# Weight pieces of a recurrent attention kernel loaded in rows of 1536 and 1280 bytes instead of 3072 and 3840

## The chip, the cores and the metric

The kernel runs on one core of a Trainium2 chip. The metric is the device time of one execution in microseconds (us); before the change it is 1880.98 us, the median of three runs. Differences below about 0.5% are not told apart from no change.

## What is computed

Two branches over 2048 tokens of width 640 are mixed by a gate. Branch A is attention with 32 heads of 192, run over 64 segments of 32 tokens; the first 8 rows of each segment's output are the memory rows of the next, so the segments form a chain. Branch B is a gated feed-forward layer.

```python
for s in range(n_seg):                                  # 64 segments, one after the other
    xs = x[:, s * seg_len:(s + 1) * seg_len, :].copy()
    h = jnp.concatenate([mem, xs], axis=1)              # 8 memory rows and 32 tokens
    q = jnp.einsum('btd,dhe->bhte', h, Wq)
    k = jnp.einsum('btd,dhe->bhte', h, Wk)
    v = jnp.einsum('btd,dhe->bhte', h, Wv)
    scores = jnp.einsum('bhqe,bhke->bhqk', q, k) * scale
    scores = jnp.where(mask[None, None], scores, -1000000000.0)
    p = _softmax(scores, axis=-1)
    o = jnp.einsum('bhqk,bhke->bhqe', p, v)
    o = jnp.einsum('bhte,hed->btd', o, Wo)
    mem = o[:, :M, :].copy()
    outs.append(o[:, M:, :])
...
return g * a + (1 - g) * b        # b = (gelu(x @ w_gate) * (x @ w_up)) @ w_down
```

## The kernel before

**Stages.** The feed-forward branch comes first (about 165 us), with its result stored in a scratch tensor. After a short stage for the left rows of the first groups the 64 segments follow, from about 180 us on, 26.4 us each on average. Everything is written as one list of operations in program order; a small scheduler (`_Sched`) splits it into one stream for each engine and puts semaphore waits where regions overlap. Each engine runs its stream in order, and so does SP, which issues nearly all DMAs.

**A segment.** The 32 heads are treated as four octets of 8 heads. For an octet, Q and K and V are products of the segment's 640 rows of h, in five slices of 128 (k = 0 to 4), with a weight piece each (`proj`, L1039 and, where the stationary operand is kept, `_matmul_kept`, L226). Then come the transposes of Q and K, scores, softmax, the transpose of p, p times V (`pv_oct`, L1172 and L1174, in products of 32 columns), and the product with Wo (`wo_split` and `wo_part`, L1201 and L1224). `PROG` interleaves the octets by hand: items `("g", i, k)` are the projections of the seven groups in `GROUPS`. Group 4 holds the Q of the fourth octet, group 5 its K, group 6 its V, and `("wo", 3, ...)` its Wo. Even segments take the octets in the order 0, 1, 2, 3, odd segments in the order 3, 2, 1, 0. Other products that fill PE (left rows, L882; left products of Wo) are interleaved too.

**Weight pieces.** A piece of Wq, Wk or Wv is one slice k of one octet: 128 partitions with a contiguous row of 1536 bf16 numbers, 3072 bytes. A piece of Wo is one head pair: 128 partitions with 3 times 640 numbers, which lie together in memory, 3840 bytes. Not all pieces fit: 17 slots are shared by a piece of octet 0 and one of octet 3 (14 of the 15 slices of Q, K and V, `NSQ = 14`, and three pairs of Wo, `NSW = 3`). As soon as the first octet of a segment has used a shared slot, the piece of its other octet is loaded there (`swap_loads`, which calls `load_piece`, L597), to be used by the fourth octet of the same segment. So each segment but the first loads 1 + 4 K pieces, 4 Q pieces, 5 V pieces and 3 Wo pieces, in the order K, Q (4), K (4), V (5), Wo (3): 14 x 393,216 + 3 x 491,520 bytes = 6.98 MB. The load of a slot waits for the PE that used it last, and PE waits for its landing. `load_piece` also makes the first loads of all resident pieces, by `load_residents`; nine pieces used once at the start are loaded to a temporary place by `load_tmp`, at another line.

**SP's stream around them.** In a segment SP issues, in this order: the first piece of K, the Q and K and V pieces as their slots come free, between them the output store of the segment before (L951) and the x load for the next (L704), later the Wo pieces, the load of the next segment's left Q and K (`stg_load`, L932), the loads of branch B's rows (L942, L947), and in most segments a store of left Q and K (L893).

Of the kernel before, what the change touches and what calls it, by code (L numbers as in the profile page):

```python
# [231 lines left out]
def _build(nc, A_x, A_mem0, A_Wq, A_Wk, A_Wv, A_Wo, seg_len, w_gate, w_up, w_down,  # L232
# [34 lines left out]
    S_ = _Sched(nc)  # L267
# [84 lines left out]
    def bview(o, nbytes, plo=0, phi=128):  # L352
        return arena[plo:phi, o // 2:(o + nbytes) // 2]
# [4 lines left out]
    def sreg(o, nbytes, plo=0, phi=128):  # L358
        return Rg("sb", o, o + nbytes, plo, phi)
# [129 lines left out]
    def piece_src(key):  # L489
        if key[0] == 3:  # L490
            return Wo2[:, key[1]]
        m, o_, k = key
        return (Wq2, Wk2, Wv2)[m][:, k, OW * o_:OW * (o_ + 1)]

    def piece_size(key):
        return GO if key[0] == 3 else GQ

    def piece_view(key, o):
        if key[0] == 3:
            return bview(o, GO).rearrange("p (c n) -> p c n", n=Dm)  # L500
        return bview(o, GQ)
# [59 lines left out]
    res_off = {}  # L561
# [8 lines left out]
    r_res = {key: sreg(o, piece_size(key)) for key, o in res_off.items()}  # L570
# [23 lines left out]

    def load_piece(key, name):
        loaded[slot_id[key]] = key
        S_.add("sp", lambda e: e.dma_start(piece_view(key, res_off[key]), piece_src(key)), writes=[r_res[key]],  # L597
               dma_sem="slot%d" % slot_id[key], name="%s %s" % (name, key))

    def piece(seg, key):  # L600
# [9 lines left out]
    def swap_loads(seg, item):  # L610
        if item[0] == "g" and item[1] == 0 and 0 < item[2] < KT - 1:
            later.extend(key for key in done_keys if key[0] == 1)
            done_keys[:] = [key for key in done_keys if key[0] != 1]
        elif later:
            done_keys[:] = sorted(done_keys + later, key=lambda key: key[:1] + key[2:])
            del later[:]
        for key in done_keys:
            other = swap_in.get(key)
            if other is None or (other in partner) == (seg % 2 == 0):
                continue  # L620
            load_piece(other, "swap s%d" % seg)
        del done_keys[:]
# [11 lines left out]
    def load_residents(cls, pick=lambda key: True):  # L634
        for key in first:
            if slot_class[key] == cls and pick(key):
                load_piece(partner[key] if key in tmp_off else key, "res")
# [39 lines left out]
    for h in range(NH):  # L677
        for w_, sb_, rw_, nm in ((w_gate, wg_sb, r_wg, "wg"), (w_up, wu_sb, r_wu, "wu")):
            S_.add("sp", lambda e, h=h, w_=w_, sb_=sb_: e.dma_start(
                sb_[h], w_.rearrange("(p k) f -> p k f", p=128)[:, :, FH * h:FH * (h + 1)]),  # L680
                writes=[rw_[h]], dma_sem="%s%d" % (nm, h))
# [758 lines left out]
```

## Time and profile before

| What | Value | Where from |
|---|---|---|
| Time, three runs | 1888.29, 1880.98, 1879.60 us | the runs |
| Time of the profiled execution | 1876.1 us | its own run |
| Its span | 1874.4 us, granted clock 0.992 | the page's first line, the view of cores |
| Segments, start to start of their piece loads | 26.4 us mean, 23.9 to 29.1 us | issues of L597 in the trace |
| Piece loads by L597 | 335 V, 330 K, 268 Q, 205 Wo: 1138 | the view of line L597 |
| Packets over 2 KB | 263,040 - 116,224 = 146,816 | the page, part 2 |

The span runs from the first to the last instruction; 1.7 us of the execution lie outside it. The packets over 2 KB are the weight pieces, 1147 loads with 128 rows each: the 1138 of L597 and the nine of `load_tmp`. In the pages, PE is the matrix engine, PEld its weight loads, DVE, ACT and POOL the vector, scalar and general engines, and SP the queue that issues DMAs. "issue" as a releaser means that the engine waited for nothing that the profile shows.

### The profile page before, as it was taken

What the parts mean: (1) busy time and instruction counts of PE and PEld (TensorE: products, weight loads), DVE (VectorE), ACT (ScalarE), POOL (GpSimd) and SP (SyncE); (2) the same over time, 40 slices, a digit from 0 to 9 for tenths busy, and PEclk for the clock granted to TensorE, in tenths of its full rate; (3) what the DMA queues carried; (4) which work ended last, traced back from release to release, by engine and by line L of the source; (5) the groups of instructions that cost most, each with busy time, mean ns of one, the idle gap of its engine ahead of it and who ended that gap; (6) DMA issues with size and microseconds to landing.
All of it is one profiled execution on the core that took longest, in us unless ns stands there. A gap on an engine that the chain in (4) does not pass through costs nothing.

```text
span 1874.4 us, 86233 instructions
## 1 busy us (share of the span) xinstructions
PE 1612.4 (86%) x42253; PEld 838.3 (45%) x34573; DVE 958.3 (51%) x2932; ACT 792.3 (42%) x1835; POOL 319.0 (17%) x1099
## 2 busy tenths in 40 slices
PE   9999889888888889888878989888888888888887
PEld 4544444444444444444434444444444444444444
DVE  2223555555555555555555555555555555555554
ACT  2223444434344444434444444444444444444433
POOL 1100111111111112111211112111111111111211
PEclk9999999999999999999999999999999999999999
DMA  9726787868777887868777887878777887878776
GB/s 341 261 56 213 295 319 274 302 247 314 288 256 275 316 314 261 297 259 319 279 252 289 320 301 261 297 276 317 279 255 291 320 303 259 293 279 313 270 268 266
DMA packets 263414, 524.72 MB, mean 280 GB/s; under 512 B 97384, under 2 KB 116224, under 8 KB 263040
## 3 DMA queue, kind: packets, MB, share of 16 engines
q1 hardware_dynamic: 259912, 516.11, 75.9%
q8 instruction: 300, 4.92, 1.0%
q10 hardware_dynamic: 3128, 3.09, 0.5%
q14 instruction: 74, 0.61, 0.1%
HBM read 498.00 MB, written 21.11 MB: 277 GB/s over the span
## 4 chain that ended last, share of the span: by engine, by line
PE 68%; issue 10%; DVE 10%; DMA 6%; ACT 6%; SPq 0%; DVEq 0%; ACTq 0%
PE ps L1039 19%; PE ps L226 14%; PE ps L1201 8%; DMA arena<-in_A_Wk_dram 3%; PE ps L799 3%; PE ps L802 3%; PE ps L1224 3%; PE ps L1172 3%; PE ps L1093 3%; PE ps L882 2%; PE ps L817 2%; DMA arena<-in_A_Wv_dram 2%; PE ps L1088 2%; PE ps L1080 2%; DVE arena L889 1%
## 5 line engine op out<-in xcount | busy, mean ns | idle before, releaser
L1039 PE MATMUL ps<-arena 128*32 128x384 bf16 x9940 | 753.1, 330 | 89.1 <-DVE arena L1344 50.2
L226 PE MATMUL ps<-arena 128*32 128x384 bf16 x7680 | 601.0, 328 | 15.6 <-ACT arena L887 5.8
L1039 PEld LDWEIGHTS ps<-arena 128*32 128x32 bf16 x9940 | 266.0, 97 | 443.8 <-issue 276.9
L1073 DVE STREAM_TRANSPOSE arena<-arena 128x384 bf16<-128x384 bf16 x512 | 278.9, 564 | 270.0 <-ACT arena L1059 269.6
L1201 PE MATMUL ps<-arena 128*32 128x320 bf16 x6144 | 309.0, 301 | 52.6 <-issue 51.3
L1059 ACT ACTIVATE arena<-ps 128x384 bf16<-128x384 f32 x512 | 236.2, 489 | 194.6 <-PE ps L1039 180.8
L1201 PEld LDWEIGHTS ps<-arena 128*32 128x32 bf16 x6144 | 176.6, 97 | 109.0 <-issue 64.8
L1107 DVE TENSOR_REDUCE arena<-ps 104x4 f32<-104x160 f32 x256 | 83.1, 325 | 199.7 <-PE ps L1093 199.1
L1119 ACT ACTIVATE ps<-ps 104x160 f32<-104x160 f32 x256 | 74.1, 289 | 251.6 <-DVE ps L1109 251.6
L1157 ACT ACTIVATE arena<-ps 128x448 bf16<-128x448 f32 x192 | 104.8, 546 | 172.9 <-PE ps L1144 172.9
L1191 POOL COPY arena<-arena 128x96 bf16<-128x96 bf16 x256 | 68.4, 267 | 583.6 <-ACT arena L1183 461.5
L936 POOL COPY arena<-arena 128x96 bf16<-128x96 bf16 x256 | 69.2, 270 | 527.4 <-PE ps L1093 442.7
L1183 ACT ACTIVATE arena<-ps 128x480 bf16<-128x480 f32 (+1 forms) x256 | 137.9, 539 | 40.5 <-PE ps L1174 33.3
L1062 ACT ACTIVATE arena<-ps 128x384 bf16<-128x384 f32 x256 | 124.8, 487 | 54.2 <-PE ps L1039 54.1
L1172 PE MATMUL ps<-arena 128*32 128x160 bf16 x3072 | 122.8, 235 | 18.4 <-issue 12.6
L882 PE MATMUL ps<-arena 128*32 128x384 bf16 x1280 | 119.1, 330 | 13.5 <-issue 13.4
L1174 PE MATMUL ps<-arena 128*32 128x64 bf16 x3072 | 110.4, 193 | 7.9 <-issue 7.7
L1172 PEld LDWEIGHTS ps<-arena 128*32 128x32 bf16 x3072 | 84.1, 96 | 69.7 <-ACT arena L1062 21.7
L1121 DVE TENSOR_REDUCE arena<-ps 104x4 f32<-104x160 f32 x256 | 82.3, 321 | 59.6 <-ACT ps L1119 53.2
L889 DVE STREAM_TRANSPOSE arena<-arena 128x384 bf16<-128x384 bf16 x128 | 73.7, 576 | 52.4 <-ACT arena L887 51.3
L887 ACT ACTIVATE arena<-ps 128x384 bf16<-128x384 f32 x128 | 62.3, 490 | 65.0 <-DVE arena L889 22.7
L1109 DVE TENSOR_TENSOR ps<-ps,arena 104x160 f32<-104x160 f32 x256 | 85.1, 332 | 8.8
(84 smaller groups left out, 1841.2 us busy)
## 6 DMA issues: line engine op xcount, KB each, us to landing
arena<-in_A_Wk_dram SPq DMA_DIRECT2D x335, 384.0 KB, 7.9
arena<-in_A_Wv_dram SPq DMA_DIRECT2D x335, 384.0 KB, 9.3
arena<-in_A_Wq_dram SPq DMA_DIRECT2D x272, 384.0 KB, 5.6
arena<-in_A_Wo_dram SPq DMA_DIRECT2D x205, 480.0 KB, 7.1
left_qk_scratch<-arena SPq DMA_DIRECT2D x64, 192.0 KB, 2.2
arena<-left_qk_scratch SPq DMA_DIRECT2D x63, 192.0 KB, 7.4
ffn_b_scratch<-arena ACTq DMA_DIRECT2D x16, 160.0 KB, 3.8
arena<-ffn_b_scratch SPq DMA_DIRECT2D x64, 40.0 KB
```

Source lines behind the costliest of these rows:

```text
L226: return e.add_instruction(mybir.InstMatmult(name=nm, start_tensor_calc=like["start"], stop_tensor_calc=stop, tile_size=(128, 32), tile_po ...
L882: fns.append(lambda e, outp=outp, rhs=rhs, j=j: e.matmul(outp, lhs, rhs, start=(k == 0), stop=(k == KT - 1), tile_position=(0, 32 * j)))
L889: S_.add("dve", lambda e: e.transpose(out=dst[:, :, m].rearrange("p q c i -> p c q i"), in_=rowl.rearrange("p (c r) -> p c r", r=L)), read ...
L1039: fns.append(lambda e, outp=outp, rhs=rhs, j=j: e.matmul(outp, lhs, rhs, start=(k == 0), stop=(k == KT - 1), tile_position=(0, 32 * j)))
L1059: S_.add("act", lambda e, m=m, bk=bk: e.activation(out=rows_sb[m], in_=ps[:, bk, 0:384], func=ACTF.Copy), reads=[r_ps[bk]], writes=[r_rows ...
L1062: S_.add("act", lambda e, i=i, bk=bk: e.activation(out=v_sb[i % NVB].rearrange("p (c n) -> p c n", c=3), in_=ps[:, bk, 0:384].rearrange("p ...
L1073: S_.add("dve", lambda e: e.transpose(out=dst[:, :, 0:L], in_=rows_sb[m].rearrange("p (c r) -> p c r", r=L)), reads=[r_rows[m]], writes=[r ...
L1157: S_.add("act", lambda e: e.activation(out=PT, in_=ps[:, bank, 0:PTW + 128], func=ACTF.Copy), reads=[r_ps[bank]], writes=[r_PT], name="pT ...
L1172: return [lambda e: e.matmul(full, v[:, e0:e0 + 32], PTm[:, j // 2], start=True, stop=False, tile_position=(0, 32 * j), skip_group_check=T ...
L1174: lambda e: e.matmul(part, vl[:, e0:e0 + 32], PTl[:, j // 2], start=False, stop=True, tile_position=(0, 32 * j), skip_group_check=True)]
L1183: S_.add("act", lambda e: e.activation(out=apx(u[:, 0, 0, :], [[R, na], [3 * R, 4], [1, R]]), in_=ps[:, A, 0:na * W].rearrange("p (c t r) ...
L1201: fns.append(lambda e, i=i, t=t, j=j, gv=gv: e.matmul(ps[32 * j:32 * j + 32, bank, 0:2 * DJ].rearrange("p (h n) -> p h n", h=2), lhs2[i], ...
```

## The change

The DMA in `load_piece` is given a limit on the contiguous part that one descriptor moves, in bytes. A row of 3072 bytes is then moved as two of 1536, and a row of 3840 bytes as three of 1280. Source, destination, order, semaphores and the number of DMAs stay. All 1138 loads of L597 are affected, the nine of `load_tmp` are not, nor any other DMA.

```diff
     def load_piece(key, name):
         loaded[slot_id[key]] = key
-        S_.add("sp", lambda e: e.dma_start(piece_view(key, res_off[key]), piece_src(key)), writes=[r_res[key]],
+        S_.add("sp", lambda e: e.dma_start(piece_view(key, res_off[key]), piece_src(key), max_dma_last_dim=1536), writes=[r_res[key]],
                dma_sem="slot%d" % slot_id[key], name="%s %s" % (name, key))
```

## The prediction, made before the changed kernel was run

> **What bounds the kernel now.** First the page's busy times, slices and DMA queues.
>
> ```profile
> PE 1612.4 (86%) x42253; PEld 838.3 (45%) x34573; DVE 958.3 (51%) x2932; ACT 792.3 (42%) x1835; POOL 319.0 (17%) x1099
> ...
> DMA  9726787868777887868777887878777887878776
> DMA packets 263414, 524.72 MB, mean 280 GB/s; under 512 B 97384, under 2 KB 116224, under 8 KB 263040
> ...
> q1 hardware_dynamic: 259912, 516.11, 75.9%
> q8 instruction: 300, 4.92, 1.0%
> ```
>
> PE is busy 86% and bounds most of the span. The DMA engines come next at 76%: within a segment they run without a pause and then rest. So the question is where a landing comes last. The list of waits tells how much PE stands for weight pieces:
>
> ```profile
> PEld ps L1039 <- issue: 276.9, 931, 2.3
> ...
> PEld ps L1039 <- DMA arena<-in_A_Wk_dram: 13.7, 28, 1.4
> ...
> PEld ps L1039 <- DMA arena<-in_A_Wv_dram: 6.7, 12, 0.9
> ...
> PE ps L1039 <- DMA arena<-in_A_Wk_dram: 5.3, 12, 1.1
> ```
>
> Columns: us in total, times, longest. These waits are small, some 20 to 30 us, but they show that there is no cover: the timeline of PE has K's matmuls of group 5 starting one by one as pieces land.
>
> ```profile
> 881.68 0.35 PE L1039 MATMUL ps<-arena 128*32 128x384 bf16 x4 [0.49 <-DMA arena<-in_A_Wk_dram]
> 882.65 0.35 PE L1039 MATMUL ps<-arena 128*32 128x384 bf16 x4 [0.62 <-DMA arena<-in_A_Wk_dram]
> 883.63 0.35 PE L1039 MATMUL ps<-arena 128*32 128x384 bf16 x4 [0.23 <-DMA arena<-in_A_Wk_dram]
> ```
>
> Starts 0.97 us apart: the pace of the DMA engines for 384 KB (about 404 GB/s). From the landings and first uses in the trace I took the slack of every piece (first use less landing; about 0.04 us when PE is waiting) in 63 segments. In 23 the smallest slack is below 0.06 us, in 18 above 1 us, in 22 between. The tight pieces are K's in group 5 and the third of Wo.
>
> The other idle time of PE is "issue", with stalls up to 2.3 us. The trace has 300 instruction packets of 16 KB, PE has 76,826 instructions, and 300 x 256 = 76,800: of 136 long stalls that end about 1.4 us after such a packet has landed, 124 come at the same remainder of the instruction count by 256. PE waits for its program. The packet starts 1.06 us (median) after PE entered the block before when the DMA engines rest, and 3.4 us when they move over 350 GB/s; 124 of 130 such stalls (138 us in the segments) are then. So under load the program waits some 2.4 us more, behind weight rows.
>
> **The change part by part.** It removes 933 x 128 rows of 3072 bytes and 205 x 128 of 3840, and adds 2 x 128 and 3 x 128 packets for each: packets go from 263,414 to 435,318. DMA instructions, bytes and order stay. SP's issue should cost nothing more: a store of 512 packets issues in 0.37 us, as a piece of 128 does.
>
> ```profile
> 868.62 0.37 SPq L893 DMA_DIRECT2D left_qk_scratch<-arena  x1
> ...
> 895.58 0.35 SPq L597 DMA_DIRECT2D arena<-in_A_Wk_dram  x1
> ```
>
> SP will stand longer at a full queue, since by estimate 100 to 130 packets an engine fill it (the first loads, issued back to back, land up to 13.9 us after issue: 14 pieces of 8 rows and a completion). Behind it are the output store, the x load and the next left Q and K (L951, L704, L932); they run behind the same pieces on the DMA engines anyway, and land a median of 3.4 us (x) and 3.3 us (left Q and K) before POOL uses them, 1.4 us at the least in the segments for the second. That covers the delays below; without that cover the whole delay of up to 1.4 us a segment would show.
>
> *Price of a split row.* By the packet records the commonest durations are 121 ns (3072 bytes), 149 (3840), 65 (1536) and 55 (1280). By these, a row costs 2 x 65 - 121 = 9 ns or 3 x 55 - 149 = 16 ns more. An engine takes 8 rows of a piece: +72 ns for Q, K or V, +128 for Wo. That is the upper end. But durations of small packets overlap: the 1280-byte rows of w_down land at 51.8 ns each (4.97 us for 96 an engine) and the 768-byte rows of w_gate and w_up at 32.6. The line through these two gives 61.4 ns for 1536; the left Q and K, eight 1536-byte rows an engine, land 486 ns (median) after the last Wo piece, 60 ns each. Sixteen at 61.4 and 7 ns for the completion are 989 ns against 975 to 979 between two V or K pieces now: +12. Without any overhead of size it is 0, the lower end for Q, K and V; against the same line for whole rows (119 ns for 3072) it is +30. I take +20, between the two. For Wo, 24 x 51.8 + 7 = 1250 against 1203 (median): +47; the line gives +61, and I take +50. Nothing in these rows makes a split row cheaper; a gain can come only by the program's wait, below.
>
> [...]
>
> *From pace to time.* The pieces of a segment stand in one queue without a pause, so piece n is late by the sum up to it: at +20 and +50, 0.16 us at the eighth (K), 0.43 us at the third of Wo. A segment grows by the largest of (delay less slack); what follows in it depends on K or Wo and goes late with it, and the next segment's loads start from its end. Over the 63 segments this is 5.0 us, in 27 of them; at 0 and +40 it is 0.3, at +30 and +61 7.9, at +72 and +128 26.5.
>
> *The program.* The loaded time of a segment grows by 14 x 0.020 + 3 x 0.050 = 0.43 us, 27 us over 64 segments. The stalls are now 138 us in about 64 x 18.5 = 1184 us of loaded time: 0.117 us for each. So 3.2 us more.
>
> *Start.* First pieces land over 100 us before use, the last of the start 1.3 us or more: nothing, covered by that slack.
>
> Sum: 5.0 + 3.2 = 8.2 us on the profiled execution's 1876.1 us (span 1874.4, 1.7 outside) = 1884.3. That execution lies 4.9 us under the median of the runs shown; on the median it is 1880.98 + 8.2 = **1889 us**, which I forecast. Its own range is 1881 to 1894 (0.3 to 12.5 us more).
>
> **Rivals.**
>
> *Durations count in full.* Each packet costs its record, +72 and +128 ns. Then pieces pace PE in 43 of 63 segments, for 26.5 us, and the loaded time grows by 1.39 us a segment, 89 us, x 0.117 = 10.4. Sum 37: 1918 us. For it: rows of 3072 now come at exactly their record (8 x 121 = 968 of 975). Against: w_down's and w_gate's rows come faster than their records of 55 and 36 ns.
>
> *The program gets through sooner (the other side).* If what stands ahead of the program's packet is a fixed number of rows, about 20 now, half-size rows halve its 2.5 us. Each stall shrinks by up to 1.3 us, in sum 126 us; PE then reaches K before its pieces do, and with +20 and +50 the same sum over segments leaves a gain of 74 us: 1807 us. It decides from a shortening of about 0.1 us a stall (-6 us net, with 13 gained). For it: the wait is there only under load. Against: where small packets stand in the queue (mean 1.9 KB), the wait is 2.6 to 2.9 us over 35 packets, and where large ones stand 2.5 us over 20; bytes (67 KB an engine) are the same and the count is not. [...]
>
> *No effect, or the split undone.* If two adjacent rows are joined again, or 1536 bytes cost nothing more (60 ns a row, as landed), the time is that of before, 1881 us. Packets of the old size in the records would show the first.
>
> **How the numbers follow.** The forecast has 0.52, the full durations 0.20, the sooner program 0.15, no effect 0.13. Within 0.5% (9.4 us) is what a measurement of this kernel can't tell from no change. The forecast's range lies across that border, and its larger part of the unknown is upward: I split it 0.25 within, 0.27 slower. Slower is 0.27 + 0.20 = 0.47; same 0.25 + 0.13 = 0.38; faster 0.15. The range for 8 in 10 goes from 1868 (a small gain at the program's stalls, and runs like those before at 1879.6) to 1920, just past the full durations; most of the sooner program's 0.15 and some above are left out.
>
> **What will show it.** Packets: 435,318, under 2 KB 433,792. Commonest durations of the new packets near 65 and 55 ns; share of q1 between 76% and 80%. Landings of K pieces 0.98 to 1.01 us apart, of Wo 1.25. PE's waits for K, V and Wo pieces grow from some 30 us to some 35 to 40; idle on "issue" grows by 3 us. The instruction packet under load still starts 3.4 us after its block. It is wrong if that start moves by more than 0.2 us either way, if K's landings stand 1.04 us apart or more, or if SP's longer standing makes x or the left Q and K late.

## The result, and the profile after

The changed kernel took 1929.43 us (median of four runs, 1927.2 to 1943.96) against 1880.29 us for the kernel before (four runs): a ratio of 1.0276, interval 1.0223 to 1.0329. It is slower, by 49 us, where the prediction had 1889 us and a range up to 1920. The profiled execution took 1930.92 us, its span is 1929.2 us.

The page of the changed kernel, its parts on busy times, slices, DMA queues and DMA issues (the last: KB of each, and median us from issue to landing):

```profile
span 1929.2 us, 86214 instructions
...
PE 1641.6 (85%) x42234; PEld 849.5 (44%) x34573; DVE 957.5 (50%) x2932; ACT 793.7 (41%) x1835; POOL 320.2 (17%) x1099
...
DMA  9727878868877888878877888868877897878787
...
DMA packets 435318, 524.72 MB, mean 272 GB/s; under 512 B 97384, under 2 KB 433792, under 8 KB 434944
...
q1 hardware_dynamic: 431816, 516.11, 79.1%
q8 instruction: 300, 4.92, 1.0%
...
arena<-in_A_Wo_dram SPq DMA_DIRECT2D x205, 480.0 KB, 7.8
```

The packets are those of the arithmetic, the bytes are the same, and the share of q1 rose from 75.9% of a shorter span to 79.1% of a longer one: 1422.7 us of engine time became 1526.0. A Wo piece lands 7.8 us after its issue; it was 7.1. PE's busy time rose by 29 us although its instructions did not change. The changed kernel's list of waits (total us, times, longest):

```profile
PEld ps L1039 <- issue: 293.4, 962, 2.3
...
PEld ps L1201 <- issue: 78.3, 58, 2.8
...
PEld ps L1039 <- DMA arena<-in_A_Wk_dram: 18.2, 42, 1.5
...
PEld ps L1039 <- DMA arena<-in_A_Wv_dram: 8.2, 17, 1.0
...
PE ps L1039 <- DMA arena<-in_A_Wk_dram: 5.2, 14, 1.1
...
PEld ps L1224 <- DMA arena<-in_A_Wo_dram: 4.1, 5, 2.1
```

The same line of L1201 in the kernel before:

```profile
PEld ps L1201 <- issue: 64.8, 45, 2.5
```

The waits for pieces grew little (K's on PEld 13.7 to 18.2 us). The waits on "issue" grew more (L1039 276.9 to 293.4, L1201 64.8 to 78.3), and these hold the stalls for the program. Lines of PE and PEld overlap, so the next table takes the time in which both stood, from the trace, by what ended it. (Where two waits end together the choice moves a few us between rows.) Its last rows are from the landings and the clock records.

| | Before | After |
|---|---|---|
| PE and PEld both idle, us | 253.2 | 278.9 |
| of it ended by "issue" | 138.9 | 160.3 |
| of it ended by a Wq, Wk, Wv or Wo piece | 9.5 | 15.6 |
| PE or PEld busy, us (half clock included) | 1613.4 | 1642.5 |
| between landings of two V / K / Wo pieces, median ns | 975 / 979 / 1203 | 1036 / 1054 / 1281.5 |
| instruction packet under over 350 GB/s: start after block entry, median us | 3.42 | 3.75 |
| lost to half clock (half the length of the stretches), us | 16.4 in 8 stretches | 50.9 in 25 |

So the DMA engines need 61 to 75 ns more for a piece of Q, K or V and 78 ns more for one of Wo. In the changed kernel's timeline of PE, a tight stretch of group 5 looks like this (start, us, and in brackets the wait before it):

```profile
899.69 0.35 PE L1039 MATMUL ps<-arena 128*32 128x384 bf16 x4 [0.27 <-DMA arena<-in_A_Wk_dram]
900.75 0.35 PE L1039 MATMUL ps<-arena 128*32 128x384 bf16 x4 [0.31 <-DMA arena<-in_A_Wk_dram]
```

The matmuls start 1.06 us apart instead of 0.97. The stalls for the program are seen in the same timeline, and what follows one of them in the view of windows (us, busy time of PE, PEld, DVE, ACT and POOL, granted clock, DMA share, GB/s):

```profile
1040.76 0.33 PE L1201 MATMUL ps<-arena 128*32 128x320 bf16 x1 [2.13 <-issue]
```

```profile
1034.20:1037.50 3.30, 3.27 (x122) 1.74 (x94) 2.45 (x9) 2.27 (x6) 0.86 (x4) 1.00 1.05 375
1037.50:1040.90 3.40, 1.27 (x35) 0.74 (x31) 1.47 (x5) 0.95 (x3) 0.27 (x1) 1.00 1.06 370
1040.90:1044.30 3.40, 3.40 (x60) 2.29 (x56) 0.00 (x0) 0.54 (x1) 0.00 (x0) 0.50 1.08 365
```

One stall of 2.13 us leaves PE busy 1.27 of 3.40 us (37%), and the next 3.40 us are granted a clock of 0.50. (The counts of matmuls in these windows, 122 and 60, are of different mixes; the matmuls of L1201 alone take 474 ns in the median inside the half-clock stretches and 299 outside.) All half-clock stretches but the last are 3.41 us long, or twice that. PE counts as busy in them: busy time inside the stretches rose from 26.5 to 90.5 us between the two profiles, and outside them it fell by 34.8, so the whole 29 us of added busy time lie there.

### The profile page after: what moved, and what is told of

Read it like the earlier page. It is cut to its first block, busy times and chain, and to the rows that moved or that the text cites. A ratio compares the mean times of both kernels' runs of the same rounds, so it can differ in the third digit from the quotient of the medians.

```text
span 1929.2 us, 86214 instructions
## 1 busy us (share of the span) xinstructions
PE 1641.6 (85%) x42234; PEld 849.5 (44%) x34573; DVE 957.5 (50%) x2932; ACT 793.7 (41%) x1835; POOL 320.2 (17%) x1099
## 3 DMA queue, kind: packets, MB, share of 16 engines
q1 hardware_dynamic: 431816, 516.11, 79.1%
## 4 chain that ended last, share of the span: by engine, by line
PE 66%; issue 10%; DVE 9%; DMA 8%; ACT 6%; SPq 0%; DVEq 0%; ACTq 0%
PE ps L1039 19%; PE ps L226 14%; PE ps L1201 8%; DMA arena<-in_A_Wk_dram 4%; PE ps L802 3%; PE ps L799 3%; DMA arena<-in_A_Wv_dram 3%; PE ps L1172 3%; PE ps L1224 2%; PE ps L1093 2%; PE ps L882 2%; PE ps L817 2%; PE ps L1088 2%; PE ps L1080 2%; DVE arena L889 1%
## 5 line engine op out<-in xcount | busy, mean ns | idle before, releaser
L1039 PE MATMUL ps<-arena 128*32 128x384 bf16 x9940 | 763.0, 334 | 92.8 <-DVE arena L1344 47.9
L1039 PEld LDWEIGHTS ps<-arena 128*32 128x32 bf16 x9940 | 267.7, 98 | 462.8 <-issue 293.4
L1201 PE MATMUL ps<-arena 128*32 128x320 bf16 x6144 | 322.2, 310 | 63.3 <-issue 61.4
L1059 ACT ACTIVATE arena<-ps 128x384 bf16<-128x384 f32 x512 | 236.2, 489 | 204.9 <-PE ps L1039 190.7
L1201 PEld LDWEIGHTS ps<-arena 128*32 128x32 bf16 x6144 | 182.1, 100 | 124.4 <-issue 78.3
L1183 ACT ACTIVATE arena<-ps 128x480 bf16<-128x480 f32 (+1 forms) x256 | 137.9, 539 | 44.2 <-PE ps L1174 37.3
L1062 ACT ACTIVATE arena<-ps 128x384 bf16<-128x384 f32 x256 | 124.9, 488 | 56.2 <-PE ps L1039 56.0
L882 PE MATMUL ps<-arena 128*32 128x384 bf16 x1280 | 118.1, 333 | 13.7 <-issue 13.7
L1172 PEld LDWEIGHTS ps<-arena 128*32 128x32 bf16 x3072 | 86.1, 97 | 69.8 <-ACT arena L1062 22.0
L1174 PEld LDWEIGHTS ps<-arena 128*32 128x32 bf16 x3072 | 84.6, 98 | 18.6 <-issue 12.7
L1139 PE MATMUL ps<-arena 104*32 104x80 bf16 x1024 | 64.4, 205 | 29.7 <-issue 13.7
```

What stands on the lines that cost most here:

```text
L882: fns.append(lambda e, outp=outp, rhs=rhs, j=j: e.matmul(outp, lhs, rhs, start=(k == 0), stop=(k == KT - 1), tile_position=(0, 32 * j)))
L1039: fns.append(lambda e, outp=outp, rhs=rhs, j=j: e.matmul(outp, lhs, rhs, start=(k == 0), stop=(k == KT - 1), tile_position=(0, 32 * j)))
L1059: S_.add("act", lambda e, m=m, bk=bk: e.activation(out=rows_sb[m], in_=ps[:, bk, 0:384], func=ACTF.Copy), reads=[r_ps[bk]], writes=[r_rows ...
L1062: S_.add("act", lambda e, i=i, bk=bk: e.activation(out=v_sb[i % NVB].rearrange("p (c n) -> p c n", c=3), in_=ps[:, bk, 0:384].rearrange("p ...
L1172: return [lambda e: e.matmul(full, v[:, e0:e0 + 32], PTm[:, j // 2], start=True, stop=False, tile_position=(0, 32 * j), skip_group_check=T ...
L1174: lambda e: e.matmul(part, vl[:, e0:e0 + 32], PTl[:, j // 2], start=False, stop=True, tile_position=(0, 32 * j), skip_group_check=True)]
```

## The experiments

All change `load_piece` (L597) of the kernel before. "Idle" below is the time in which PE and PEld both stood; unchanged kernels ran beside each group.

**Which pieces.** The split for Q, K and V alone (first added line), then for Wo alone (second; `key[0]` is 3 for Wo).

```diff
-        S_.add("sp", lambda e: e.dma_start(piece_view(key, res_off[key]), piece_src(key)), writes=[r_res[key]],
+        S_.add("sp", lambda e: e.dma_start(piece_view(key, res_off[key]), piece_src(key), max_dma_last_dim=4096 if key[0] == 3 else 1536), writes=[r_res[key]],
...
+        S_.add("sp", lambda e: e.dma_start(piece_view(key, res_off[key]), piece_src(key), max_dma_last_dim=1536 if key[0] == 3 else 4096), writes=[r_res[key]],
```

> Rows of Q, K and V split, rows of Wo whole. Pace theory (a split row takes an engine longer, everything else follows from the longer transfers): the 14 pieces of a segment land 0.065 us later each, 0.91 us of the 1.14 us that the full change adds to a segment's transfers, so about 39 of its 49 us: 1915 to 1924 us, with landings of K pieces 1.05 us apart and of Wo pieces 1.20 as before. If what counts is the packets in the queue (of 435,318 some 80% of the added ones stay), the same; this run only measures the share of Q, K and V.

> Rows of Wo split into three, all others whole. Pace theory: 3 pieces, 0.078 us each, 0.23 us a segment: about +10 us, 1886 to 1894 us, K landings 0.975 us apart as before. Packet-count theory (each added packet costs the same somewhere else than on the engines): 410 of the 1343 added packets in a thousand per... that is 52,480 of 171,904 added packets, 31%, so +15 us.

Measured: 1915.01 us, ratio 1.0190 (1.0151 to 1.0228), and 1898.51 us, ratio 1.0105 (1.0062 to 1.0147), against 1879.11. Alone the parts give 35.9 and 19.4 us, in sum 55 for 49 together: they add up within their intervals. Landings moved only where rows were split (K 1052 ns and Wo 1197 in the first; K 978 and Wo 1274 in the second). Idle on issue was 164.0 and 157.5 us, idle on pieces 13.9 and 3.7. The first came as expected, at the lower edge of its range. The second was 4 us over the top of the pace theory's range and nearer to the packet-count theory's +15 us, so this run alone does not decide between the two. Wo's split adds 3 x 71 ns = 0.21 us a segment, 14 us in all, and costs 19. PE did not stand longer for pieces (3.7 us, 9.5 before) but for its program (157.5, 138.9 before). Why the cost is more than the delay is open.

**Only the first loads.**

```diff
-        S_.add("sp", lambda e: e.dma_start(piece_view(key, res_off[key]), piece_src(key)), writes=[r_res[key]],
+        S_.add("sp", lambda e: e.dma_start(piece_view(key, res_off[key]), piece_src(key), max_dma_last_dim=1536 if name == "res" else 4096), writes=[r_res[key]],
```

> Only the first loads of the resident pieces are split, the loads within the segments are whole. Pace theory: these have over 1 us of slack, so 1878 to 1886 us, although the landings before 61 us show the slower pace (1.05 us instead of 0.98); about 8 windows of half clock as before. If the half-clock windows of the changed kernel were a matter of the chip or of the hour, this run would show about 25 of them and some 30 us more.

Measured: 1879.44 us, ratio 0.9997 (0.9975 to 1.0020). The window in which only first loads run, in the view of windows, of the kernel before and then of this one:

```profile
32.00:44.00 12.00, 11.71 (x113) 6.89 (x112) 2.72 (x6) 3.29 (x6) 0.30 (x1) 1.00 1.03 403
```

```profile
32.00:44.00 12.00, 11.60 (x113) 6.95 (x114) 2.32 (x6) 3.29 (x6) 0.30 (x1) 1.00 1.06 376
```

With nothing else to disturb them, rows of 1536 bytes move at 376 GB/s where rows of 3072 move at 403 (last column). That is the price of the row, 7%, seen by itself, and it costs no time where PE does not wait. In this profile 37.0 us were lost to half clock in 20 stretches, more than double the 16.4 us in 8 of before, in a run only 8.5 us longer (1884.58 us): lost clock is not paid in full. The 20 stretches are not the "about 8" that was expected. So the number of stretches differs much between executions of equally fast kernels, and not all of the rise from 8 to 25 belongs to the change.

**Smaller still.** 768 bytes: four packets for a Q, K or V row, five for Wo.

```diff
-        S_.add("sp", lambda e: e.dma_start(piece_view(key, res_off[key]), piece_src(key)), writes=[r_res[key]],
+        S_.add("sp", lambda e: e.dma_start(piece_view(key, res_off[key]), piece_src(key), max_dma_last_dim=768), writes=[r_res[key]],
```

> All rows of the piece loads cut to 768 bytes: four packets for Q, K and V, five for Wo. By the record of a 768-byte packet (36 ns) a Q, K or V piece takes 8 x 4 x 36 + 9 = 1.16 us (+0.18) and a Wo piece 8 x 5 x 36 + 9 = 1.45 (+0.25), 3.3 us more a segment: at the change's rate (49 us for 1.14 us a segment) +140 us, about 2020 us. By the landings of the gate and up weights (32.6 ns a packet) it is 1.05 and 1.31 us, 1.4 us a segment, +60 us, about 1940 us. If the change's cost came from 1536 bytes as such and not from packet overhead, this would be no slower than the change, 1929 us.

Measured: 1974.33 us, ratio 1.0518 (1.0499 to 1.0537), between the two. K landed 1194 ns apart, Wo 1458. A K piece gives an engine 8 more packets in the changed kernel (+75 ns) and 24 more here (+215): about 9 ns for each packet added in both. For Wo, 16 and 32 more, it is 5 and 8 ns. From the page and the waits of this kernel:

```profile
q1 hardware_dynamic: 723144, 516.11, 87.4%
```

```profile
PEld ps L1039 <- DMA arena<-in_A_Wk_dram: 56.7, 91, 1.4
PEld ps L1224 <- DMA arena<-in_A_Wo_dram: 53.1, 53, 1.9
PEld ps L1201 <- issue: 43.1, 45, 3.2
```

Now the pieces come last: idle on pieces is 115 us, and on issue only 103. The likely reading, not shown stall by stall, is that the program arrives while PE waits for a piece, so that the two waits stand in for each other.

**Packets or bytes.** Rows left whole, but after every fourth piece of the segments a DMA of 80 rows of 1280 bytes is moved from x to a scratch tensor, which slows the pieces by bytes, with few packets.

```diff
+    pace = [0]
+    pace_scr = nc.dram_tensor("pace_scratch", (300, 80, Dm), BF, kind="Internal").ap()
...
+        pace[0] += 1
+        if name != "res" and pace[0] % 4 == 0:
+            n = pace[0] // 4
+            S_.add("sp", lambda e: e.dma_start(pace_scr[n], x2[0:80, :]), dma_sem="pace", watch=True, name="pace %d" % n)
```

> All rows whole, but after every fourth piece load in the segments SP issues one more DMA, 80 rows of 1280 bytes from the input x to a scratch tensor that nobody reads: five rows an engine, about 0.28 us of engine time, 1.2 us a segment, as much as the split costs. Pace theory: the time goes where the split's goes, 1920 to 1945 us, with some 20 to 30 windows of half clock and idle of PE on issue near 160 us. If small packets cost by their number or by how the engines change queues, this adds only 4,300 x 5 packets and the time stays within 1880 to 1895 us.

Measured: 1914.84 us, ratio 1.0197 (1.0148 to 1.0246). Each added DMA went as 16 packets of 6400 bytes (five rows joined) and 16 completions. With 8,608 more packets it costs as much as the first experiment with 119,424 more. So a longer queue costs that much with few packets too; that packets cost nothing besides is not shown, and the run also adds issues on SP and writes to the scratch tensor. The time is 5 us under the pace theory's range, and it was not paid as expected: idle on issue stayed at 133.2 us, idle on pieces rose to 47.7, and there were 17 half-clock stretches.

```profile
PEld ps L1046 <- DMA arena<-in_A_Wk_dram: 45.1, 81, 2.1
PEld ps L1046 <- DMA arena<-in_A_Wv_dram: 25.9, 42, 1.9
PEld ps L1231 <- DMA arena<-in_A_Wo_dram: 15.5, 18, 1.6
```

(These are L1039 and L1224 of before, seven lines lower.) The extra bytes come in lumps ahead of certain pieces, and there the piece is the last to arrive.

**Without the load.** In the segments each piece moves only 16 of its 128 rows, whole and then split.

```diff
+        rows = 128 if name == "res" else 16
+        S_.add("sp", lambda e: e.dma_start(piece_view(key, res_off[key])[0:rows], piece_src(key)[0:rows]), writes=[r_res[key]],
...
+        S_.add("sp", lambda e: e.dma_start(piece_view(key, res_off[key])[0:rows], piece_src(key)[0:rows], max_dma_last_dim=1536), writes=[r_res[key]],
```

> Rows whole; the piece loads within the segments move 16 of the 128 rows only, so 7/8 of the shared weights stay those of the other octet. Theory: the program of PE no longer waits behind weight rows, so the stalls on issue (139 us) nearly go, with the 9 us of waits for pieces and the windows of half clock (16 us lost): 1715 to 1740 us. If the program's stalls had nothing to do with weight loads, 1865 to 1880 us.

> As the run with an eighth of the rows in the segments (7/8 of the shared weights stay those of the other octet), with every row split as in the change. Theory: with the engines resting most of the time the pace of a row does not matter: within 5 us of the unsplit one. If split rows cost on SP or by DMA instruction, some 30 us or more remain.

Measured: 1711.76 us, ratio 0.9116 (0.9100 to 0.9133), and 1712.34 us, ratio 0.9122 (0.9108 to 0.9136). The split costs nothing here, as expected, so no cost comes with the DMA instruction as such. The first is 3 us under its expected range. Its page:

```profile
span 1711.9 us, 86233 instructions
...
PE 1577.1 (92%) x42253; PEld 810.6 (47%) x34573; DVE 956.3 (56%) x2932; ACT 791.8 (46%) x1835; POOL 319.4 (19%) x1099
```

Idle on issue fell from 139 to 1.8 us, idle on pieces to nothing, and half clock to two stretches. The profiled span is 162 us shorter than before: 137 us less idle on issue, 9.5 us less on late pieces and 36 us less busy time of PE or PEld (1613.4 to 1577.9), against 20 us more of other idle time.

**Fewer pieces in flight.** If the program waits behind what is queued, a shorter queue should help. A piece's issue is made to wait for the landing of the one n before it (here n = 3; the split ones have the limit on row size too).

```diff
+    inflight = []
...
+        op = S_.add("sp", lambda e: e.dma_start(piece_view(key, res_off[key]), piece_src(key)), writes=[r_res[key]],
                dma_sem="slot%d" % slot_id[key], name="%s %s" % (name, key))
+        if name != "res":
+            if len(inflight) >= 3:
+                op.deps.add(inflight[-3])
+            inflight.append(op)
```

> All rows whole, at most two pieces in flight. Theory: the program's stalls nearly go (below 40 us), but two pieces in some 3 us from issue to landing is 1.5 us a piece, 25 us for 17: pieces become the bound, waits of PE for them over 150 us, 1930 to 2000 us.

> All rows whole; within the segments SP issues a piece only when the third piece before it has landed, so that at most three are in flight. Theory (PE's program waits behind a fixed amount, about 67 KB an engine, of weight rows that stand ahead of it): with three pieces in flight at most 2 x 24 KB stand ahead and less than that in the queue of an engine, so the program packet starts some 2 us after its block instead of 3.4, and the stalls on issue fall from 139 us to below 90. Pieces keep near 1 us apart if issue to landing stays near 3 us. Then 1800 to 1860 us; if the pieces come later than that, waits for them eat the gain. If the program waits because HBM or the engines are busy, and not for what is queued, the stalls stay at 139 us and the time is 1880 us or more.

> All rows whole, at most four pieces in flight. Theory: up to 3 x 24 KB queued, near the fixed amount, so the program gains less: stalls on issue 110 to 139 us, pieces at the full pace, 1850 to 1880 us. By the other view 1880 us.

> All rows whole, at most five pieces in flight. With four in flight the stalls on issue fell from 139 to 15 us and the waits for pieces rose from 10 to 160. Theory: with five the pieces keep the engines' pace more often, so waits for pieces of 30 to 100 us and stalls on issue of 30 to 80 us, in sum no more than the 149 us of before: 1840 to 1885 us. If the waits for pieces under a limit came from SP's order alone, and not from too few in flight, they stay above 120 us and the time above 1900 us.

> All rows whole, at most six pieces in flight. Theory: between five and no limit: stalls on issue 60 to 120 us, waits for pieces 15 to 50 us, 1850 to 1882 us.

> All rows whole, at most eight pieces in flight. Theory: nearly the order of before, since issue to landing is 7.5 us in the median (some seven pieces): stalls on issue 120 to 140 us, 1870 to 1885 us.

> At most three pieces in flight, rows split as in the change. Theory: the program's wait is short whatever the rows, so that part of the split's cost (some 22 of 49 us) goes, and the later pieces remain: 15 to 35 us more than the same with whole rows. If the split's cost has nothing to do with the program's wait, 45 to 55 us more than with whole rows.

> At most six pieces in flight, rows split as in the change. Theory (the split's cost is the engines' slower pace, paid either at the program's stalls or at waits for pieces, whichever ends last): 35 to 55 us more than with whole rows at the same limit, but more of it in waits for pieces and less in stalls on issue. If the cost were mostly the program's longer wait, it falls below 30 us here.

| Pieces in flight, rows | us | Ratio (interval) | Idle on issue / on pieces, us | Program's wait under load, median us |
|---|---|---|---|---|
| 2, whole | 2602.40 | 1.3805 (1.3764 to 1.3846) | - / 616 | - |
| 3, whole | 2104.30 | 1.1166 (1.1137 to 1.1194) | 3.8 / 291 | 0.81 |
| 4, whole | 1910.92 | 1.0139 (1.0116 to 1.0163) | 14.6 / 160 | 1.07 |
| 5, whole | 1862.33 | 0.9924 (0.9895 to 0.9953) | 83.6 / 40.6 | 1.72 |
| 6, whole | 1864.27 | 0.9917 (0.9890 to 0.9944) | 123.1 / 6.2 | 2.12 |
| 8, whole | 1878.56 | 0.9994 (0.9977 to 1.0012) | 137.9 / 4.2 | 2.41 |
| no limit, whole | 1880.29 | 1 | 138.9 / 9.5 | 2.51 |
| 3, split | 2146.74 | 1.1384 (1.1341 to 1.1427) | 1.2 / 339 | - |
| 6, split | 1906.05 | 1.0144 (1.0120 to 1.0168) | 136.2 / 32.1 | 2.06 |
| no limit, split | 1929.43 | 1.0276 (1.0223 to 1.0329) | 160.3 / 15.6 | 2.66 |

The program's wait (from 1.06 us after block entry to the start of its packet, where the engines go on at over 280 GB/s in the 0.6 us after) does fall with the pieces in flight, so the stalls are made by the queue. With two to four in flight the expectations on time were far off: in the kernel before a single piece took 2.9 us or more from issue to landing, and with so few under way the pieces come late. With five, idle on pieces falls to 40.6 us, so the order of SP's stream alone, which the limit changes too, is not what made them late (that would have left over 120 us). Between them lies a small gain: five and six beat the kernel before by 0.8%, both intervals below 1. The waits with four and with six pieces (L1045 and L1230 are L1039 and L1224 of before):

```profile
PEld ps L1045 <- DMA arena<-in_A_Wv_dram: 126.8, 147, 2.3
...
PEld ps L1230 <- DMA arena<-in_A_Wo_dram: 73.9, 80, 2.5
...
PEld ps L1207 <- issue: 9.9, 24, 1.8
```

```profile
PEld ps L1207 <- issue: 65.6, 43, 3.4
...
PEld ps L1045 <- DMA arena<-in_A_Wv_dram: 4.1, 8, 0.9
PEld ps L1230 <- DMA arena<-in_A_Wo_dram: 3.5, 7, 0.7
```

Six in flight with split rows answers a further question. The program's wait is no longer than with whole rows (2.06 and 2.12 us), yet the split costs 42 us there too, as it does at three in flight (42 us, where 15 to 35 were expected if a short program's wait takes its part away). In the profiles of the two at six, idle on pieces grows by 26 us, on issue by 13, and lost clock from 14.9 to 30.4 us. So the price is in the slower transfer, and it is paid at whichever comes last.

## Why the prediction was wrong

**What failed: the price of a split row.** The prediction took "+20" for a Q, K or V piece and "+50" for Wo; the landings give +61 to +75 and +78, which is +6.3% to +7.7% for Q, K and V and +6.5% for Wo. At +65 and +78 its own sum over the segments gives 21 us for late pieces instead of 5.0, and its rule for the program 8.5 instead of 3.2: some 30 us, or 1911, instead of 8.2. The packet records, kept as the upper end (+72, +128), were right for Q, K and V and too high for Wo. The rows used against them, 60 ns for the left Q and K and 51.8 for w_down, were other DMAs; they still land at that pace (left Q and K after Wo: 486 ns before, 495 after) while split weight rows of the same 1536 bytes take 65 (1036 and 1054 ns for 16). Why is open: source, destination and neighbours differ, and that was not tried. One of the signs that the prediction had named for being wrong, K's landings 1.04 us apart or more, came with 1.054.

**The program's term was mis-sized: 3.2 us forecast, 21 measured.** Its rule was that stalls grow with the loaded time. With the measured 14 x 0.065 + 3 x 0.078 = 1.14 us a segment that rule gives 64 x 1.14 x 0.117 = 8.5 us, still too little. What grew is each stall: there are 132 in the profile before and 133 after, 139.9 and 161.9 us in sum, 0.16 us longer each. The wait behind the weight rows went from 2.51 to 2.66 us in the median and from 2.67 to 2.88 in the upper quartile, in step with the slower bytes. The upper quartile of bytes an engine moves meanwhile is the same, 66.8 and 66.6 KB; the median count of rows went from 19 to 42. The start after block entry moved by 0.33 us, past the 0.2 that the prediction had set.

**Late pieces: 5.0 us forecast, 6.1 measured as idle.** This is right by chance, since the true prices would have given 21 us. A likely reason why so little of it shows is that PE stands for the program longer too, and so comes later to the pieces; this was not followed segment by segment.

**Left out: the half clock.** The profiled pair differs by 54.8 us of span: 25.7 of idle time and 29.1 of busy time. The prediction had no term for the second. It lies in the half-clock stretches, 34.5 us more of lost clock. But the profiled execution of before lost less than most, and so the pair shows more of it than the medians do. How much of the 49 us between medians is due to it is not settled: over 29 executions of the kernel before and of kernels equally fast, the time rises by 0.48 us for each us lost (correlation 0.64); the mean loss went from 24.3 us (15 to 37 in single executions) to 42.5 (29 to 54 in the four of the changed kernel), which would make some 9 us if the loss is the cause. Idle on issue and on pieces make 27 together; the remaining 13 or so are not attributed.

**Rivals.** "Durations count in full" (1918 us) had the right price for Q, K and V, too high a one for Wo, and the same two terms; it fell short for the program and the clock. "The program gets through sooner" fell: the wait grew. "No effect" fell: the packets have the new sizes, with records of 65 and 55 ns, and a K piece takes 75 ns more.

**Right:** the direction as likelier than the others, the packets, the commonest durations, a share of q1 between 76% and 80%, that the start costs nothing, and that SP's longer standing harms nothing on PE's path: the x loads land 3.1 us and the left Q and K 3.0 us (medians) before POOL uses them, where it was 3.4 and 3.3. SP does stand longer (the median L597 issue of V went from 522 to 601 ns), and branch B's rows came late for POOL (L968 waited 19.4 us for them instead of 5.3), off the path. Its issue itself was not free: the shortest went from 322 to 362 ns.

## What to carry to other kernels

Price a new DMA row size by a stretch of the same transfer, as the run that split only the first loads did (403 to 376 GB/s), rather than by landings of other DMAs. The packet records were right within 11 ns for a piece of Q, K or V, but 50 ns too high for one of Wo. Here, with q1's packets at 75.9% of the engines' time, the slower transfer was also paid by PE's own instruction stream (idle on issue 138.9 to 160.3 us), and with rows of 768 bytes idle on issue fell to 103 us while idle on pieces rose to 115, so sum neither alone. Try a limit on the loads in flight: with six pieces of 384 to 480 KB the data stayed on time, with five some of it came late, and both gained 0.8%.

## What the runs showed of the hardware that was not expected

- Half clock came after windows of 3.41 us in which PE was busy for a share of 0.26 to 0.63 (profile after), the longest stall in them being 1.1 to 2.5 us. On the grid of the clock records all 16 windows with a share under 0.43 were followed by half clock, and 9 of the 73 from 0.43 to 0.63; in the profile before it is 3 of 3 and 5 of 66. What decides in between is open.
- An instruction packet waits behind about 67 KB of rows an engine (upper quartile), with rows of 3072 and of 1536 bytes alike (and 68 in the run with extra bytes). With 768-byte rows it was 50 KB, 66 rows, and the median wait 1.98 us. So it is neither a count of rows nor bytes alone; what sets it is open.
- Removing seven eighths of the weight rows in the segments took idle on issue from 139 to 1.8 us: nearly all of the program's stalls are made by the load.
